# Half A's weights: one clamp of the weight conversion moves from VectorE in PSUM to GpSimd in SBUF

## The chip, the cores and the metric

The kernel runs on one core of a Trainium2 chip. The metric is the device time of one execution in microseconds (us). Such times are given as the median of several runs; a separate execution was profiled, and every row below is from that one.

## The reference

The inputs are q, k, v (batch 4, 8 heads, 576 positions, 64 per head), a threshold tau, and four weight matrices, moe_w_in and moe2_w_in (512 x 2048) and moe_w_out and moe2_w_out (2048 x 512). The matrices arrive as float64, and the kernel reads each number as a pair of 32-bit words. What is computed:

```
scores = (q @ k^T) / sqrt(64);  keep those >= rowmax - tau, set the others to -1e9
attn   = exp(scores - rowmax);  attn /= sum(attn) + 1e-9;  x = (attn @ v) as (2304, 512)
h = x @ w_in;    g = h * clip(h + 3, 0, 6) / 6;   x = g @ w_out
h = x @ w2_in;   g = h - tanh(h);                 out = g @ w2_out
```

## The kernel before

TensorE multiplies each number as a high and a low part, so every product is three passes.

**Stages.** Attention runs over 144 units, each one block of 128 queries (or a left-over block) of one head. For a unit TensorE makes the scores (L678) into one of two PSUM score buffers `s`. VectorE takes the row maximum (L683), ScalarE the exponential into `e` (L685), and VectorE masks it against the threshold (L694), which is the last reader of the score buffer. Two units form a group: ScalarE rounds the group's probabilities to a high half `pp` (L699), GpSimd subtracts to get the low half (L705), SP issues a transposing DMA into `pt` (L708), and TensorE multiplies with v (L731). The first feed-forward layer's hidden units are split into half A (1024 of them) and half B. Half A runs between the attention units (`layer1`, L489 and L850), as batches of queries become complete. Half B and the second feed-forward layer follow after the attention, from about 480 us.

**Half A's weights.** They come as 16 blocks, 8 of `w_in` (tiles `ai`) and 8 of `w_out` (tiles `ao`), each 128 x 512 numbers of 64 bits. `load_w` (L388) converts one block. SP loads the raw words into `st` (3 buffers, L406 and L411). ScalarE writes the magnitude of the upper words, taken as float32 (L414). Four VectorE steps follow: a clamp of the magnitude to the range of float32 (L418), a shift with a mask (L420), sign and exponent from the raw upper word (L423), and the last bits from the lower word, back into `st` (L426). `hi_lo` then splits the float32 number: ScalarE writes the high part (L448), GpSimd the low part (L451). For half A the magnitude and the steps L418 to L423 live in a PSUM buffer `m` (`scratch=R_m`, two buffers, shared with the products of `layer1`). For all other weights they live in `wu` in SBUF (`R_wu`, two buffers), and those blocks come later than 480 us.

**Order of the work.** Every operation is recorded with `add` as a task with an engine, an assumed duration, a key and what it reads and writes. `Plan.issue` then simulates the engines with these durations, lets each free engine take the ready task with the lowest key, and writes the instructions in the order in which they start. Each engine afterwards executes its own list in exactly that order and waits at an instruction whose inputs aren't there. A duration or a dependency that changes can thus move any later instruction of any engine. Half A's blocks have keys that place them among the attention units. The assumed durations that bear on the change are 0.65 us for a VectorE step of half A and `t_pool(512)` = 0.14 + 512 x 0.0021 = 1.215 us for a GpSimd pass over 512 elements.

Of the kernel before, what the change touches and what calls it, by code (L numbers as in the profile page):

```python
# [9 lines left out]
F32 = mybir.dt.float32  # L10
F32R = mybir.dt.float32r
F16 = mybir.dt.float16
I32 = mybir.dt.int32
U32 = mybir.dt.uint32
BF16 = mybir.dt.bfloat16
ACTF = mybir.ActivationFunctionType
ALU = mybir.AluOpType
# [55 lines left out]
class Plan:  # L73
# [13 lines left out]
    def add(self, eng, dur, key, fn, r=(), w=(), after=(), xfer=0.0, hold=False, slack=0.0, port=None):  # L87
        r, w = ([getattr(b, "of", b) for b in x] for x in (r, w))
        deps = dict.fromkeys(after)
        for b in r:  # L90
            deps.update(dict.fromkeys(b.writers))
        t = Task(eng, dur, key, fn, deps, xfer, hold, slack, eng == "pool" if port is None else port)
        t.w = w
        users = dict.fromkeys((*r, *w))
        t.free = [b for b in users if b.ring.free]
        for b in users:
            b.users.append(t)
        for b in w:
            b.writers.append(t)
        self.tasks.append(t)  # L100
        return t
# [86 lines left out]
def t_act(n, sbuf=False, scalars=False):  # L188
    return 0.05 + n / 1200.0 + 0.043 * sbuf + 0.094 * scalars
# [6 lines left out]
def t_pool(n):  # L196
    return 0.14 + n * 0.0021
# [3 lines left out]
def attention_moe_moe_kernel(  # L201
# [29 lines left out]
    nc = tc.nc  # L231
    B, H, S, D = q.shape
    DM = H * D
# [12 lines left out]
    TINY = 2.0 ** -15  # L246
    HUGE = 122879.9921875
# [8 lines left out]
    add = plan.add  # L256
# [122 lines left out]
    R_wu = Ring(2, lambda i: st_p.tile([128, DM], I32, tag=f"wu{i}", name="wu"), free=True)  # L379
# [8 lines left out]
    def load_w(kind, m, src, key, step, to, after=(), slack=0.0, scratch=None, cs=0.0, first=None, low="pool",  # L388
               found=None, put=None):

        wst, wu = R_st.new(), (scratch or R_wu).new()
        f0 = m * 128
        raw = lambda i: wst.t.rearrange("p (n t) -> p n t", t=2)[:, :, i]  # L400
        part = lambda dt: wu.t.bitcast(dt)
        split_, staged = isinstance(to, list), isinstance(to, (Buf, View))

        def load():
            if kind == "i":
                nc.sync.dma_start(  # L406
                    out=wst.t.rearrange("p (k n) -> p k n", k=KD),
                    in_=src[:, 2 * f0:2 * (f0 + 128)].rearrange("(k p) f -> p k f", p=128),
                )
            else:  # L410
                nc.sync.dma_start(out=wst.t, in_=src[f0:f0 + 128, :])  # L411

        add("dma", 0.47, key, load, w=[wst], after=after, xfer=1.75, slack=slack)
        add("act", t_act(DM, sbuf=True), key + 3, lambda: nc.scalar.activation(  # L414
            out=part(F32), in_=raw(1).bitcast(F32), func=ACTF.Abs), r=[wst], w=[wu, to] if staged else [wu],
            slack=cs if first is None else first)
        steps = [
            lambda: nc.vector.tensor_scalar(  # L418
                out=part(F32), in0=part(F32), scalar1=TINY, scalar2=HUGE, op0=ALU.max, op1=ALU.min),
            lambda: nc.vector.tensor_scalar(  # L420
                out=part(I32), in0=part(I32), scalar1=3, scalar2=0x3FFFFFF8,
                op0=ALU.logical_shift_left, op1=ALU.bitwise_and),
            lambda: nc.vector.scalar_tensor_tensor(  # L423
                out=part(I32), in0=raw(1), scalar=-0x40000000, in1=part(I32),
                op0=ALU.bitwise_and, op1=ALU.bitwise_or),
            lambda: nc.vector.scalar_tensor_tensor(  # L426
                out=raw(1).bitcast(U32) if split_ else to.t.bitcast(U32) if staged else part(U32), in0=raw(0).bitcast(U32), scalar=29, in1=part(U32),
                op0=ALU.logical_shift_right, op1=ALU.bitwise_or),
        ]
        for n, f in enumerate(steps):  # L430
            add("dve", 0.65 if n > 1 or scratch else 0.5, key + 3 + n * step, f,
                r=[wu] if n < 2 else [wu, wst], w=[wst] if n == 3 and split_ else [to] if n == 3 and staged else [wu], slack=cs, port=not scratch)
        if staged:
            return wu
        if not split_:
            if found is not None:
                found(wu, key + 3 + 4 * step)
            return add("dma", 0.47, key + 3 + 4 * step, lambda: nc.sync.dma_start(out=to, in_=part(F32)), r=[wu], xfer=0.8)
        n = DM // len(to)
        for h, W in enumerate(to):  # L440
            f32 = lambda h=h: raw(1)[:, h * n:(h + 1) * n].bitcast(F32)
            (hi_lo if put is None else put)(f32, W, [wst], key + 3 + 4 * step, step, n, cs, low)
        return to
# [421 lines left out]
    with tc.manual_schedule():  # L865
# [4 lines left out]
            out=tau_b[:, 2:3], in0=tau_b[:, 0:1], scalar1=0.0, scalar2=scale, op0=ALU.is_ge, op1=ALU.mult,  # L870
# [72 lines left out]
        for u in range(NU + LAG + XL + 4):  # L943
            if u >= LOOK and (u - LOOK) % LOOKS == 0 and wb_parts:
                look(*wb_parts.pop(0), when(u), pend[u - 6].writers[-1:])
            while rounds and rounds[0][0] <= u:
                at_u, r = rounds.pop(0)
                record_round(r, when(at_u))
            if wa_parts:
                kind, m = wa_parts.pop(0)  # L950
                n = 2 * MH - len(wa_parts) - 1
                WA[kind, m] = load_w(
                    kind, m, w1_in if kind == "i" else w1_out, T0 + STEP * (W0 + WS * n + WO * (kind == "o")), 0.8,
                    [R_w[kind, m].new()], slack=ST, scratch=R_m, cs=CS)[0]
            if u < NU:
                pend[u] = softmax(u, when(u))
            if 0 <= u - LAG < NU and sum_group(u - LAG)[-1] == u - LAG:
                weighted(u - LAG, when(u) + PVK, pend[u - LAG])
# [132 lines left out]
        for kind in "io":  # L1091
            mx, k0 = wmax["b" + kind], start - FW - 6.0
            top = add("dve", 0.15, k0, lambda mx=mx: nc.vector.tensor_reduce(
                out=mx[:, 0:1], in_=mx[:, 5:5 + MH], axis=AX.X, op=ALU.max), after=seen[kind])
# [41 lines left out]
        for o, (kind, src) in enumerate((("i", w1_in), ("o", w1_out))):  # L1136
            for m in range(MH):
                W = WB[kind, m] = (R_bw if kind == "i" else R_bo).new()
                load_w(kind, MH + m, src, start - FW + WBO + WBS * (MH * o + m), 0.8, [W], late, cs=CB, first=CB1,
                       put=scaled_pair(wmax["b" + kind][:, 2:3], scaled["b" + kind], kind == "o"))  # L1140
        key = T2
# [7 lines left out]
        for i, ms in work:  # L1149
            c, n = blocks[i]  # L1150
# [21 lines left out]
            if ms[-1] == MH - 1:  # L1172
                y = load_y(i, key - 10.0)
                for h in range(KD // 2):
                    last = add("dve", t_dve(2 * n, scalars=True), key + 2 * PM, lambda h=h, y=y, acc=acc, n=n, i=i: nc.vector.scalar_tensor_tensor(  # L1175
                        out=y.t[:, 2 * h:2 * h + 2, 0:n], in0=acc[h].t[:, 0:2 * n].rearrange("p (d n) -> p d n", d=2),
                        scalar=unscale[:, 1, i:i + 1], in1=y.t[:, 2 * h:2 * h + 2, 0:n], op0=ALU.mult, op1=ALU.add),
                        r=[acc[h], y], w=[y], after=x_ready[i][1])
# [6 lines left out]
                    out=y2[i], in_=y.t[:, :, 0:n]), r=[y], xfer=1.5)  # L1185
# [30 lines left out]
        def to_dram(i, gate, key):  # L1216
            kind, m = wd_parts[i]
            q = quarter(m)
            mx, c = wmax[f"{kind}{q}"], m % (2 * MQ)

            def found(wu, k):
                f32 = lambda: wu.t.bitcast(F32)
                junk = View(R_t2.new(), lambda t: t.bitcast(BF16)[:, 0:DM])
                x = row_sums(f32, mx[:, 5 + c:6 + c], lambda: junk.t, [wu], [junk], k, DM, CL)
                w_found.setdefault((kind, q), []).append(x)

            wd_stores[kind, m] = load_w(
                kind, m, w2_in if kind == "i" else w2_out, key, 0.8, wd[kind, m], [gate], slack=0.2, cs=CL, first=CF,
                found=found)
# [237 lines left out]
        for idx, st in enumerate(order2):  # L1467
# [7 lines left out]
            n = NB  # L1475
# [121 lines left out]
```

## Time and profile before

| | |
|---|---|
| three timed runs | 1088.57, 1094.69, 1092.71 us; median 1092.71 |
| the profiled execution | 1088.51 us; its span from first to last instruction 1086.7 us |
| TensorE matmul busy | 1015.0 us (93%) |
| VectorE busy | 847.6 us (78%) |
| ScalarE busy | 718.6 us (66%) |
| GpSimd busy | 339.0 us (31%) |
| mean granted TensorE clock | 0.964 |

PE is TensorE's matmul, PEld its weight load, DVE VectorE, ACT ScalarE, POOL GpSimd, SP the engine that issues most DMAs. Busy shares are averages over stages with different limits. The page cuts the span into 40 equal slices of 27.2 us and gives each engine's busy share in tenths, and the granted TensorE clock in tenths of full speed:

```profile
PE   5668799999999899988999999999999999999998
DVE  5889977687869788758797778889976796784564
ACT  6867979687967786645675566756755675574332
POOL 2656757666855675623000000000001111121000
PEclk8668899999999989998999999999999999999999
```

### The profile page before, as it was taken

To read this page: it belongs to the slowest core of one execution; us is meant where nothing else is said; L and a number is where in the kernel's file an instruction comes from. 1 tells how busy PE (TensorE), PEld (TensorE's weight loads), DVE (VectorE), ACT (ScalarE), POOL (GpSimd) and SP (SyncE) were. 2 spreads that over 40 slices of the span, in tenths; PEclk is the share of its full clock that TensorE was granted. 3 is DMA by queue.
4 is the path that set the end of the run, shared out by engine and by line. 5 is a ranking of instruction groups with operands and counts; after the bars stand their busy time and mean duration, and the time that the engine had idled before them with its cause. 6 is when DMAs were issued, how large, how long until landed. Compare 5 with 4: busy or idle time off the path is not lost.

```text
span 1086.7 us, 23294 instructions
## 1 busy us (share of the span) xinstructions
PE 1015.0 (93%) x8984; PEld 838.6 (77%) x8984; DVE 847.6 (78%) x1630; ACT 718.6 (66%) x1312; POOL 339.0 (31%) x353
## 2 busy tenths in 40 slices
PE   5668799999999899988999999999999999999998
PEld 4557788998999799978988888876676666666664
DVE  5889977687869788758797778889976796784564
ACT  6867979687967786645675566756755675574332
POOL 2656757666855675623000000000001111121000
PEclk8668899999999989998999999999999999999999
DMA  7899688967899989978657755432333866573335
GB/s 184 165 222 213 132 159 182 196 132 158 187 181 192 205 175 216 219 159 261 201 173 257 253 199 185 165 108 97 107 117 118 208 131 117 126 127 51 87 92 142
DMA packets 285007, 179.27 MB, mean 165 GB/s; under 512 B 202976, under 2 KB 257760, under 8 KB 284896
## 3 DMA queue, kind: packets, MB, share of 16 engines
q1 hardware_dynamic: 279088, 168.07, 61.0%
q0 software_dynamic: 5184, 9.44, 6.5%
q8 instruction: 71, 1.16, 0.5%
q14 instruction: 40, 0.33, 0.1%
q10 hardware_dynamic: 624, 0.26, 0.1%
HBM read 89.13 MB, written 46.14 MB: 124 GB/s over the span
## 4 chain that ended last, share of the span: by engine, by line
PE 58%; DVE 4%; ACT 1%; DMA 1%; issue 0%; SPq 0%; ACTq 0%; DVEq 0%
PE ya L489 24%; PE m L489 16%; PE h L489 10%; PE m L850 3%; PE s L678 2%; PE tp L731 1%; DMA y<-y 1%; PE h L850 1%; PE m L476 0%; DVE x L1276 0%; DMA st<-in_moe_w_in_dram 0%; DVE xh L1048 0%; DVE t L803 0%; PE tp L561 0%; DVE y L1175 0%
## 5 line engine op out<-in xcount | busy, mean ns | idle before, releaser
L705 POOL TENSOR_TENSOR pp<-e,pp 128x128 f16<-128x128 f32 (+3 forms) x156 | 181.1, 1182 | 120.3 <-issue 54.1
L489 PE MATMUL ya<-wo,g 128*128 128x512 f16 x864 | 205.4, 379 | 1.0 <-DVE g L813 0.6
L489 PEld LDWEIGHTS <-wi 128*128 128x128 f16 x1536 | 150.0, 98 | 40.4
L1416 POOL DMA_DIRECT2D po<-o x36 | 31.2, 876 | 459.7 <-ACT o L1410 459.7
L489 PEld LDWEIGHTS <-g 128*128 128x128 f16 x864 | 84.1, 98 | 79.3 <-DVE g L813 1.1
L683 DVE TENSOR_REDUCE z<-s 128x1 f32<-128x576 f32 x144 | 107.9, 753 | 45.4 <-PE s L678 44.7
L694 DVE SCALAR_TENSOR_TENSOR e<-s,z,e 128x576 f32<-128x576 f32 x144 | 115.8, 811 | 22.1 <-ACT e L685 17.1
L678 PE MATMUL s<-ks,q 128*128 128x288 f32 x512 | 105.9, 337 | 20.9 <-DVE e L694 20.1
L685 ACT ACTIVATE e<-s,z 128x576 f32<-128x576 f32 x144 | 105.0, 739 | 26.6 <-DVE z L683 20.3
L489 PE MATMUL m<-xT,ai 128*128 128x256 f32 (+1 forms) x720 | 112.8, 301 | 1.8 <-DVE st L426 0.6
L678 PEld LDWEIGHTS s<-ks,q 128*128 128x128 f32 x512 | 82.4, 212 | 29.4 <-DVE e L694 13.4
L489 PEld LDWEIGHTS m<-xT,ai 128*128 128x128 f32 x720 | 99.3, 190 | 3.7 <-DVE st L426 1.1
L489 PE MATMUL ya<-g,bo 128*128 128x256 f16 x864 | 101.1, 273 | 0.5 <-DVE g L813 0.5
L731 PE MATMUL tp<-vt,pt 128*128 128x65 f16 (+1 forms) x2240 | 88.4, 199 | 8.5 <-ACT q L591 2.4
L489 PE MATMUL m<-x,wi 128*128 128x256 f16 x768 | 95.2, 273 | 0.0
L731 PEld LDWEIGHTS <-pt 128*128 128x128 f16 (+1 forms) x2240 | 79.8, 104 | 16.7 <-DMA pt<-pp 6.0
L1381 ACT ACTIVATE t<-t,hid_s 128x512 f32<-128x512 f32 x72 | 51.6, 718 | 62.0 <-DVE t L1372 61.4
L489 PEld LDWEIGHTS <-bo 128*128 128x128 f16 x864 | 84.1, 98 | 10.6 <-issue 0.9
L489 PEld LDWEIGHTS <-bw 128*128 128x128 f16 x864 | 84.1, 98 | 10.4 <-issue 0.4
L813 DVE SCALAR_TENSOR_TENSOR g<-g,t 128x512 f16<-128x512 f16 x108 | 73.8, 686 | 20.7 <-ACT g L809 20.2
L809 ACT ACTIVATE g<-t 128x512 f16<-128x512 f32 x108 | 67.0, 624 | 33.7 <-DVE t L1383 26.0
L699 ACT ACTIVATE pp<-e 128x1152 f16<-128x1152 f32 (+1 forms) x80 | 85.1, 1064 | 5.0 <-DVE e L694 4.7
(177 smaller groups left out, 1878.0 us busy)
## 6 DMA issues: line engine op xcount, KB each, us to landing
st<-in_moe_w_in_dram SPq DMA_DIRECT2D x40, 512.0 KB, 5.0
st<-in_moe_w_out_dram SPq DMA_DIRECT2D x40, 512.0 KB, 4.4
xf<-xs SPq DMA_DIRECT2D x18, 512.0 KB, 5.2
y<-y SPq DMA_DIRECT2D x18, 512.0 KB, 3.8
po<-o POOLq DMA_DIRECT2D x36, 256.0 KB, 4.2
xs<-xT SPq DMA_DIRECT2D x8, 640.0 KB, 4.9
y<-ys SPq DMA_DIRECT2D x9, 512.0 KB, 5.9
po<-o SPq DMA_DIRECT2D x18, 256.0 KB, 2.0
```

The lines of the kernel that those rows point to most:

```text
L489: nc.tensor.matmul(ps, l[a], r[b], start=first and t == 0 and i == 0, stop=last and t == 2 and i == n - 1,)
L678: nc.tensor.matmul(ps.t[:, half, 0:SH], l, ks[:, half * SH:(half + 1) * SH], start=i == 0, stop=i == len(ops) - 1,)
L683: add("dve", 0.69, key, lambda: nc.vector.tensor_reduce(out=z.t[:, 0:1], in_=s(), axis=AX.XY, op=ALU.max, negate=True), r=[ps], w=[z])
L685: exp = add("act", 0.66, key, lambda: nc.scalar.activation(out=ex(), in_=s(), func=ACTF.Exp, bias=z.t[:, 0:1]), r=[ps, z], w=[e])
L694: add("dve", 0.74, key, lambda: nc.vector.scalar_tensor_tensor(out=ex(), in0=s(), scalar=z.t[:, 1:2], in1=ex(), op0=ALU.is_ge, op1=ALU.mul ...
L699: high = add("act", t_act(w * S, sbuf=True), key, lambda: nc.scalar.activation(out=pp.t[:, 0:w, 0:S], in_=e.t[:, 0:w, :], func=ACTF.Copy), ...
L705: add(eng, dur, key, lambda src=src, dst=dst, queue=queue: queue.tensor_tensor(out=pp.t[:, 0:w, dst], in0=e.t[:, 0:w, src], in1=pp.t[:, 0: ...
L731: nc.tensor.matmul(pv.t[0:m, w_ * (D + 1):(w_ + 1) * (D + 1)], pt.t[:, n, blk, rows], vv, start=o == 0, stop=o == len(ops) - 1)
L809: hi = add("act", t_act(n, sbuf=True), key, lambda: nc.scalar.activation(out=gh(), in_=t(), func=ACTF.Copy, scale=GS2 if far else 1.0), r= ...
L813: go = lambda: nc.vector.scalar_tensor_tensor(out=gl(), in0=gh(), scalar=1.0 / GS2, in1=t(), op0=ALU.mult, op1=ALU.subtract)
L850: prev = [add("pe", t_mm(n, 1), kd, lambda p=p, l=l, r=r, m=m, s=s, ps=ps: nc.tensor.matmul(ps.t[:, 0:n], W["o", m].t[:, l, s], r[m].t[:, ...
L1381: add("act", t_act(2 * NB, sbuf=True, scalars=True), key, lambda: nc.scalar.activation(out=s_(), in_=h.t, func=ACTF.Tanh, scale=c), r=[h], ...
```

## The change

For half A alone (`scratch` given) the magnitude gets a tile of its own, `mag`, from the SBUF ring `R_wu`. ScalarE writes it there. The clamp is one GpSimd instruction in place in that tile, its minimum first and its maximum second. The VectorE clamp L418 is left out for half A, and the shift reads `mag` and writes the PSUM buffer, which half A takes from that step on. For all other weights `mag` is `wu`, and nothing differs.

```diff
         wst, wu = R_st.new(), (scratch or R_wu).new()
+        mag = R_wu.new() if scratch else wu
...
+        size = lambda dt: mag.t.bitcast(dt)
         add("act", t_act(DM, sbuf=True), key + 3, lambda: nc.scalar.activation(
-            out=part(F32), in_=raw(1).bitcast(F32), func=ACTF.Abs), r=[wst], w=[wu, to] if staged else [wu],
+            out=size(F32), in_=raw(1).bitcast(F32), func=ACTF.Abs), r=[wst], w=[mag, to] if staged else [mag],
             slack=cs if first is None else first)
+        if scratch:
+            add("pool", t_pool(DM), key + 3, lambda: nc.gpsimd.tensor_scalar(
+                out=size(F32), in0=size(F32), scalar1=HUGE, scalar2=TINY, op0=ALU.min, op1=ALU.max), r=[mag], w=[mag])
         steps = [
-            lambda: nc.vector.tensor_scalar(
+            None if scratch else lambda: nc.vector.tensor_scalar(
                 out=part(F32), in0=part(F32), scalar1=TINY, scalar2=HUGE, op0=ALU.max, op1=ALU.min),
             lambda: nc.vector.tensor_scalar(
-                out=part(I32), in0=part(I32), scalar1=3, scalar2=0x3FFFFFF8,
+                out=part(I32), in0=size(I32), scalar1=3, scalar2=0x3FFFFFF8,
                 op0=ALU.logical_shift_left, op1=ALU.bitwise_and),
...
         for n, f in enumerate(steps):
+            if f is None:
+                continue
             add("dve", 0.65 if n > 1 or scratch else 0.5, key + 3 + n * step, f,
-                r=[wu] if n < 2 else [wu, wst], w=[wst] if n == 3 and split_ else [to] if n == 3 and staged else [wu], slack=cs, port=not scratch)
+                r=[mag] if n < 2 else [wu, wst], w=[wst] if n == 3 and split_ else [to] if n == 3 and staged else [wu], slack=cs, port=not scratch)
```

## Rows read from the trace of the kernel before

**Rows 1.** Stretches: length, busy us of each engine (instructions), clock, DMA share, GB/s.
```profile
20.00:140.00 120.00, 88.50 (x825) 77.19 (x826) 107.86 (x181) 96.03 (x194) 80.84 (x76) 0.74 0.83 175
140.00:480.00 340.00, 325.46 (x3665) 309.02 (x3663) 261.81 (x511) 257.16 (x492) 210.65 (x213) 0.99 0.87 181
480.00:1086.70 606.70, 591.53 (x4458) 444.96 (x4458) 468.51 (x916) 353.69 (x607) 43.91 (x46) 0.99 0.54 152
```

**Rows 2.** The same view in slices of 20 us: PE, PEld, DVE, ACT, POOL.
```profile
40.00:60.00 20.00, 13.60 (x118) 11.94 (x118) 16.80 (x29) 16.01 (x32) 15.20 (x13) 0.66 0.99 198
60.00:80.00 20.00, 12.46 (x90) 10.58 (x90) 17.75 (x28) 13.01 (x26) 10.81 (x10) 0.57 0.96 214
80.00:100.00 20.00, 15.09 (x158) 13.05 (x159) 18.27 (x30) 14.69 (x29) 13.94 (x14) 0.74 0.86 200
100.00:120.00 20.00, 17.69 (x192) 15.85 (x192) 19.63 (x34) 17.96 (x43) 14.78 (x15) 1.00 0.93 191
120.00:140.00 20.00, 14.64 (x165) 13.87 (x164) 16.59 (x29) 16.14 (x34) 14.79 (x15) 0.83 0.62 113
```

**Rows 3.** Waits of PE and DVE, 20 to 140: us in total, times, longest.
```profile
PE s L678 <- DVE e L694: 18.9, 13, 4.9
...
DVE z L683 <- PE s L678: 3.2, 10, 0.8
DVE m L418 <- ACT m L414: 2.8, 3, 1.6
```

**Rows 4.** Lines L418, L426: ns min/median/max, first and last start, form.
```profile
L418 DVE TENSOR_SCALAR wu<-wu x48: 404/419/524, 487.5 to 923.5; 128x512 f32<-128x512 f32 x48
L418 DVE TENSOR_SCALAR m<-m x16: 680/690/700, 23.3 to 127.8; 128x512 f32<-128x512 f32 x16
...
L426 DVE SCALAR_TENSOR_TENSOR st<-st,m x16: 629/677/680, 34.4 to 132.0; 128x512 uint32<-128x512 uint32 x16
```

**Rows 5.** VectorE in order of time: start us, us, instruction.
```profile
76.20 0.69 DVE L418 TENSOR_SCALAR m<-m 128x512 f32<-128x512 f32 x1
76.80 0.81 DVE L694 SCALAR_TENSOR_TENSOR e<-s,z,e 128x576 f32<-128x576 f32 x1
```

**Rows 6.** GpSimd's groups, 20 to 140: busy us, mean ns | idle before.
```profile
L705 POOL TENSOR_TENSOR pp<-e,pp 128x1024 f16<-128x1024 f32 x16 | 34.2, 2138 | 0.0
L451 POOL TENSOR_TENSOR ao<-st,ao 128x512 fp32r<-128x512 f32 x8 | 10.5, 1308 | 5.3 <-ACT ao L448 5.3
...
L705 POOL TENSOR_TENSOR pp<-e,pp 128x512 f16<-128x512 f32 x3 | 3.5, 1163 | 0.0
L554 POOL COPY qr<-qr 128x256 f32<-128x256 f32 x8 | 3.2, 404 | 0.0
```

**Rows 7.** Waits of SP's queue, 20 to 140.
```profile
SPq L708 <- POOL pp L705: 3.9, 4, 1.6
```

**Rows 8.** ScalarE: the two forms of L414, and a wait, 20 to 140.
```profile
L414 ACT ACTIVATE wu<-st x48: 648/666/704, 486.8 to 922.4; 128x512 f32<-128x512 f32 x48
L414 ACT ACTIVATE m<-st x16: 608/624/647, 19.9 to 127.0; 128x512 f32<-128x512 f32 x16
...
ACT e L685 <- POOL pp L705: 2.0, 2, 1.3
```

**Rows 9.** Waits of GpSimd for ScalarE and VectorE, 20 to 140.
```profile
POOL pp L705 <- ACT pp L699: 10.0, 4, 5.2
POOL gl L816 <- ACT gh L809: 5.5, 5, 2.2
POOL ao L451 <- ACT ao L448: 5.3, 4, 2.5
POOL ai L451 <- ACT ai L448: 4.6, 4, 2.1
...
POOL vt L644 <- ACT vt L642: 0.7, 1, 0.7
POOL x L778 <- DVE rx L766: 0.5, 1, 0.5
```

## The prediction

> **What bounds the kernel now.** I read three views in turn: busy time by stretch, then the waits inside the stretch that the change touches, then the order of instructions on single engines.
>
> Busy time first [rows 1]. From 140 us on, TensorE is the bound: 325.46 of 340 us busy until 480, and 591.53 of the 606.7 us after it, both at a granted clock of 0.99. Nothing of half A's weight work lies there, so the change can alter that part only by letting it begin sooner or later. The stretch from 20 to 140 us is another kernel: TensorE 88.50 of 120 us, VectorE 107.86, ScalarE 96.03, GpSimd 80.84. The reader is to see that VectorE is the fullest engine, and, slice by slice, that it leads in each of the five slices from 40 us on, with 16.59 to 19.63 us of 20 [rows 2]. TensorE's granted clock is 0.57 to 0.74 in the first three of them, a mean between its levels of 1.2 and 2.4 GHz.
>
> The waits say the same. In this stretch TensorE's scores wait 18.9 us for VectorE's masking step L694, 13 times, because that step gives the score buffers back; VectorE's own longest waits are 3.2 and 2.8 us in sum [rows 3]. So VectorE sets the pace of the attention units up to 140 us, TensorE sets it afterwards, and the 16 weight blocks of half A lie wholly inside the first part: L418 runs from 23.3 to 127.8 us [rows 4].
>
> **The change, part by part.**
>
> *Removed.* 16 VectorE clamps in PSUM, of 690 ns median [rows 4]. An instruction on this engine begins before the records let its predecessor end: the clamp at 76.20 is followed by the next instruction at 76.80 [rows 5], so one clamp takes 0.60 us of the queue. 16 x 0.60 = 9.6 us. VectorE was busy for 107.86 of 120 us, 90%; I count 90% of this as path, 8.6 us.
>
> *Added on GpSimd.* 16 one-input passes of 128x512 float32 in SBUF. No row shows this operation. The nearest is the copy L554, 128x256 float32 in 404 ns: also one input, one output, half the size. Doubled it gives 0.81 us. With a fixed part taken off it is less: the two sizes of L705, 1163 ns for 512 and 2138 ns for 1024 elements, differ by 1.90 ns per element and leave 0.19 us fixed, so the copy costs 0.84 ns per element and 512 of them 0.62 us. The upper bound is the two-input subtraction of the same shape, L451 with 1308 ns [rows 6]. A second arithmetic step rides in the same pass; I take 0.75 us, near the copy, and keep 0.62 to 1.31. 16 x 0.75 = 12.0 us on an engine that is idle for 39.2 of the 120 us. Below nothing it can't be: the engine gains work and loses none.
>
> The Trainium skill's "GPSIMD Engine Reference", section "Engine selection", speaks against such a move: elementwise work belongs on VectorE, GpSimd being about twice as slow with two inputs, though near line rate with one. Its section "Elementwise — side-by-side cycle accounting" gives 769 ns for 512 elements in its best loop, by which the 16 would be 12.3 us, an estimate from that page; no run here shows it.
>
> *The wait that moves.* VectorE waited 2.8 us, three times, for the magnitudes [rows 3]. That wait now falls on GpSimd, which takes its work in a written order: behind a clamp that waits for L414 stand the low halves of the probabilities (L705), the low halves of the weights (L451) and the query copies (L554). For L705 wait the transposing DMAs of SP, which wait 3.9 us on it now [rows 7], and behind those the next loads of SP, q, k and the raw weights among them; ScalarE's exponentials L685 wait for L705 to give back its e buffer, 2.0 us in two waits [rows 8]. I expect this last wait to double, and charge 2.0 us. VectorE's shift L420 gets a wait for GpSimd instead of ScalarE. Behind it on VectorE stand the softmax steps L683 and L694, so a late clamp stalls them; the written order puts the shift where a clamp of 1.2 us is done, more than I assume, and I charge nothing. If that cover fails, each late clamp costs up to its own 0.75 us.
>
> *Rerouted operands.* The magnitudes go to SBUF instead of PSUM: 666 against 624 ns [rows 8], 16 x 0.042 = 0.7 us on ScalarE, which is 80% busy and hides it. The shift L420 now reads SBUF and writes PSUM. With both ends in PSUM such a step takes 690 ns, with both in SBUF 419 [rows 4]; the mixed case is not shown. I take the first, no change; the second would give 16 x 0.27 = 4.3 us more. Half A's PSUM buffer is held from the shift instead of from the magnitudes, which can only free it earlier for layer 1, whose products share the two buffers; I count nothing for it. The two SBUF buffers of the magnitudes are otherwise used from 486.8 us on [rows 8], so no one else waits for them.
>
> The Trainium skill's "VectorE: DVE Perf Modes", section "Why PSUM operands drop a tier", holds that any PSUM operand keeps float32 at the single rate. The two forms of L418 agree with it at their ends, 419 and 690 ns; by it the mixed shift stays at the slow price and the extra 4.3 us don't come.
>
> *Sum.* 8.6 - 2.0 = 6.6 us earlier at 140 us. After that TensorE is 96% and 98% busy [rows 1] on work that stays the same, so I let the gain pass to the end whole. The profiled execution took 1088.51 us (its span of 1086.7 and 1.8 around it): 1081.9. The median of the three timed runs is 1092.71, 4.2 above the profiled one; I forecast against the median: 1086.1, as 1086.
>
> **The rivals.**
>
> *GpSimd ties VectorE, nothing moves.* GpSimd's idle 39.2 us are not all free. 26.6 of them are waits for ScalarE and VectorE in six lines, 10.0 + 5.5 + 5.3 + 4.6 + 0.7 + 0.5 [rows 9]. If those waits stay as long, 12.6 us are free, and 16 clamps at 0.79 us fill them: the stretch keeps its 120 us although VectorE got lighter. 1092.7. For it speaks how close 0.79 lies to 0.75; against it that most of these waits are for producers that VectorE itself holds up, and so should shrink.
>
> *GpSimd becomes the bound: slower.* The same queue, with the clamp at the price of L451. 16 x 1.31 = 20.9 us against 12.6 free: the stretch grows by 8.3 us, to 1101.0. The place is L705 behind the clamps, seen as waits of L685 and of the transposes. It decides from 0.79 us per clamp upward if the waits stay. For it: in the slice from 40 to 60 us GpSimd is at 15.20 of 20 and gets three clamps, 3.9 us at that price, so 19.1; from 100 to 120, 14.78 and 3.9 [rows 2]. Against it: one input instead of two.
>
> *The shift gets cheap too.* Should L420 run at its SBUF price, 4.3 us come on top: 1081.8. Nothing shows VectorE at that rate with one end in PSUM.
>
> *The change does less than it says.* All later instructions are placed anew by the planner from its own prices, so layer 1's products may fall otherwise among the units. TensorE idles for 31.5 us between 20 and 140 and for 14.5 until 480 [rows 1]; an order that is worse by a few waits of 1 to 2 us blurs every case. I hold that in the widths, not as a case.
>
> **How the numbers follow.** The forecast has 0.46, its own range 1080 to 1091; the tie 0.29; the slower case 0.19; the cheap shift 0.06. About 0.5%, 5.5 us, is what a measurement of this kernel can tell from no change: faster than 1087.2 are the cheap shift and 0.40 of the forecast, 0.46; within it the tie and 0.06 of the forecast, 0.35; slower than 1098.2 the last case, 0.19. The range 1077 to 1100 leaves out about half of the slower case and a little below the cheap shift.
>
> **What would show it right or wrong.** Right: VectorE's busy time from 20 us to the last ao block falls by some 11 us, that last block is done about 6 us sooner than now (its L426 begins at 132.0 us, [rows 4]), and the stretch behind it has the same length. The clamp's mean shows which case holds: under 0.79 us the first two, above it the slower. Wrong in its main step if VectorE's busy share in this stretch drops well below 90% with no gain in time, its idle time ended by GpSimd or by TensorE's scores; wrong in its second if the stretch gets shorter and the part after 140 us gives it back. It fails outright if L685 or the transposes wait more than 8 us for L705.

## The result and the profile after

The changed kernel took 1105.91 us (median of 4 runs, 1103.27 to 1107.32) against 1091.55 us of the kernel before on the same chip (4 runs): a ratio of 1.0139, 95% interval 1.0110 to 1.0169. It is slower by 1.4%. The forecast was 1086 us with a range of 1077 to 1100. The profiled execution took 1103.27 us, with a span of 1101.5 (before 1086.7).

In the changed kernel's line numbers the magnitude is L416, the clamp L420, the shift L425 and the last bits L431; scores, row maximum, exponential and mask are L685, L690, L692 and L701; layer 1's first products (x with `ai`) are L496, its second ones (the gated result with `ao`) L857. The four weight lines first, from the view of one line: instruction and count, ns min/median/max, first and last start.

```profile
L416 ACT ACTIVATE wu<-st x16: 652/661/682, 20.2 to 135.2; 128x512 f32<-128x512 f32 x16
...
L420 POOL TENSOR_SCALAR wu<-wu x16: 610/613/619, 20.9 to 136.6; 128x512 f32<-128x512 f32 x16
...
L425 DVE TENSOR_SCALAR m<-wu x16: 676/684/695, 23.6 to 138.5; 128x512 int32<-128x512 int32 x16
...
L431 DVE SCALAR_TENSOR_TENSOR st<-st,m x16: 678/679/690, 31.1 to 140.6; 128x512 uint32<-128x512 uint32 x16
```

The moved clamp is cheap and the shift costs what it did. But L431 begins for the last time at 140.6 us, where [rows 4] had 132.0. Busy time by stretch, the rows that answer to [rows 1], and one part of them:

```profile
20.00:140.00 120.00, 88.45 (x784) 78.43 (x784) 101.24 (x170) 98.30 (x197) 87.18 (x91) 0.74 0.82 181
140.00:480.00 340.00, 319.63 (x3540) 303.65 (x3541) 254.93 (x493) 249.33 (x478) 211.04 (x213) 0.97 0.83 174
480.00:1101.50 621.50, 604.80 (x4622) 457.97 (x4620) 477.40 (x930) 359.05 (x618) 44.72 (x48) 0.99 0.54 151
...
140.00:180.00 40.00, 35.43 (x363) 34.08 (x364) 21.86 (x40) 24.95 (x53) 19.93 (x19) 0.87 0.65 142
```

The last row has this counterpart in the kernel before:

```profile
140.00:180.00 40.00, 38.30 (x432) 35.90 (x430) 30.55 (x55) 34.54 (x74) 24.70 (x24) 1.00 0.82 179
```

VectorE lost 6.6 us of work up to 140 us, and TensorE is exactly as busy there as before, 88.45 against 88.50 at 0.74. Most of the loss is right behind: from 140 to 180 us TensorE is busy for 35.43 instead of 38.30 us, at a granted clock of 0.87 instead of 1.00. Busy time times clock is 30.8 against 38.3 us, so 7.5 us of full-speed work are missing. From 180 to 480 us TensorE is busy for another 3 us less, 284.20 against 287.16 us, at the same clock of 0.99. The units say the same. Counted by the starts of the row maximum, with the first unit as number 0, unit 28 is 2.5 us ahead of the kernel before, unit 36 is 2.6 us behind, unit 44 is 10.0 behind, the last one 11.9 and the end 14.8. The waits from 20 to 140 us, for [rows 3]:

```profile
DVE z L690 <- PE s L685: 9.8, 13, 1.9
...
PE s L685 <- DVE e L701: 15.8, 18, 2.6
```

VectorE now waits 9.8 us for scores, not 3.2. What happens at 140 us is seen in the order of time, TensorE first (start, us, instruction; in brackets the idle time before it and what ended it):

```profile
140.73 0.80 PE L685 MATMUL s<-ks,q 128*128 128x288 f32 x4 [2.23 <-DVE e L701]
143.65 3.38 PE L738 MATMUL tp<-vt,pt 128*64 128x65 f16 x56 [2.12 <-DVE ks L593]
146.84 3.25 PE L857 MATMUL m<-gh,ao 128*128 128x256 f32 x16
149.93 1.12 PE L857 MATMUL m<-gl,ao 128*128 128x256 f32 x8
150.89 2.08 PE L857 MATMUL m<-gh,ao 128*128 128x256 f32 x16
...
154.71 0.69 PE L685 MATMUL s<-ks,q 128*128 128x288 f32 x4
```

```profile
142.02 0.76 DVE L690 TENSOR_REDUCE z<-s 128x1 f32<-128x576 f32 x1
...
154.55 0.68 DVE L770 SCALAR_TENSOR_TENSOR rx<-x,sv 128x16 f32<-128x16 f32 x1 [7.82 <-ACT x L745]
...
155.43 0.76 DVE L690 TENSOR_REDUCE z<-s 128x1 f32<-128x576 f32 x1
```

And TensorE in the kernel before, at its first second products:

```profile
136.69 2.15 PE L850 MATMUL m<-gh,ao 128*128 128x256 f32 x16
138.68 1.12 PE L850 MATMUL m<-gl,ao 128*128 128x256 f32 x8
139.63 0.69 PE L678 MATMUL s<-ks,q 128*128 128x288 f32 x4
140.16 1.35 PE L850 MATMUL m<-gh,ao 128*128 128x256 f32 x10
```

Before, scores stand between the second products. After, the second products begin 10 us later, the first 16 of them take 3.25 instead of 2.15 us, and no scores come from 140.73 to 154.71: a hole of 13.4 us between the maxima of two units, 142.02 to 155.43. The longest hole of the kernel before among units 30 to 48 is 7.6 us. This hole is a sight, not yet a cause; s1 below tests it.

### The profile page after: what moved, and what is told of

It reads as the page before. It is cut to its first block, busy times and chain, and to the rows that moved or that the text cites. A ratio compares the mean times of both kernels' runs of the same rounds, so it can differ in the third digit from the quotient of the medians.

```text
span 1101.5 us, 23287 instructions
## 1 busy us (share of the span) xinstructions
PE 1022.7 (93%) x8984; PEld 847.8 (77%) x8984; DVE 842.7 (77%) x1614; ACT 718.2 (65%) x1312; POOL 346.5 (31%) x369
## 4 chain that ended last, share of the span: by engine, by line
PE 75%; DVE 5%; ACT 4%; DMA 1%; issue 1%; POOL 1%; SPq 0%; ACTq 0%; POOLq 0%; DVEq 0%
PE ya L496 24%; PE m L496 19%; PE h L496 10%; PE m L857 8%; PE s L685 5%; PE tp L738 4%; PE tp L568 1%; DVE z L690 1%; PE h L857 1%; DVE e L701 1%; ACT e L692 1%; PE m L483 1%; DMA pt<-pp 1%; DMA f<-wdi 1%; ACT pp L706 0%
## 5 line engine op out<-in xcount | busy, mean ns | idle before, releaser
L712 POOL TENSOR_TENSOR pp<-e,pp 128x128 f16<-128x128 f32 (+3 forms) x156 | 180.9, 1180 | 120.1 <-ACT pp L706 57.9
L496 PE MATMUL ya<-wo,g 128*128 128x512 f16 x864 | 205.4, 379 | 1.4 <-ACT g L816 0.8
L496 PEld LDWEIGHTS <-wi 128*128 128x128 f16 x1536 | 150.0, 98 | 40.4
L690 DVE TENSOR_REDUCE z<-s 128x1 f32<-128x576 f32 x144 | 108.1, 754 | 53.7 <-PE s L685 52.3
L496 PEld LDWEIGHTS <-g 128*128 128x128 f16 x864 | 84.1, 98 | 79.6 <-ACT g L816 1.2
L701 DVE SCALAR_TENSOR_TENSOR e<-s,z,e 128x576 f32<-128x576 f32 x144 | 116.3, 812 | 22.8 <-ACT e L692 10.7
L685 PE MATMUL s<-ks,q 128*128 128x288 f32 x512 | 107.8, 339 | 25.7 <-DVE e L701 25.3
L692 ACT ACTIVATE e<-s,z 128x576 f32<-128x576 f32 x144 | 105.2, 738 | 24.8 <-DVE z L690 20.2
L496 PE MATMUL m<-xT,ai 128*128 128x256 f32 (+1 forms) x720 | 114.3, 304 | 2.5 <-DVE t L810 1.1
L685 PEld LDWEIGHTS s<-ks,q 128*128 128x128 f32 x512 | 84.2, 215 | 33.8 <-DVE e L701 17.6
L496 PEld LDWEIGHTS m<-xT,ai 128*128 128x128 f32 x720 | 101.0, 193 | 4.2 <-DVE t L810 2.0
L738 PE MATMUL tp<-vt,pt 128*128 128x65 f16 (+1 forms) x2240 | 91.5, 202 | 12.9 <-DVE q L600 2.9
L496 PE MATMUL ya<-g,bo 128*128 128x256 f16 x864 | 101.6, 273 | 0.7 <-DVE g L820 0.7
L738 PEld LDWEIGHTS <-pt 128*128 128x128 f16 (+1 forms) x2240 | 82.7, 106 | 21.5 <-issue 10.6
L496 PE MATMUL m<-x,wi 128*128 128x256 f16 x768 | 95.2, 273 | 0.0
L496 PEld LDWEIGHTS <-bo 128*128 128x128 f16 x864 | 83.8, 98 | 10.8 <-issue 1.1
L496 PEld LDWEIGHTS <-bw 128*128 128x128 f16 x864 | 84.4, 98 | 10.0
L816 ACT ACTIVATE g<-t 128x512 f16<-128x512 f32 x108 | 66.9, 624 | 30.8 <-DVE t L1390 26.1
```

The source lines that it names most:

```text
L496: nc.tensor.matmul(ps, l[a], r[b], start=first and t == 0 and i == 0, stop=last and t == 2 and i == n - 1,)
L685: nc.tensor.matmul(ps.t[:, half, 0:SH], l, ks[:, half * SH:(half + 1) * SH], start=i == 0, stop=i == len(ops) - 1,)
L690: add("dve", 0.69, key, lambda: nc.vector.tensor_reduce(out=z.t[:, 0:1], in_=s(), axis=AX.XY, op=ALU.max, negate=True), r=[ps], w=[z])
L692: exp = add("act", 0.66, key, lambda: nc.scalar.activation(out=ex(), in_=s(), func=ACTF.Exp, bias=z.t[:, 0:1]), r=[ps, z], w=[e])
L701: add("dve", 0.74, key, lambda: nc.vector.scalar_tensor_tensor(out=ex(), in0=s(), scalar=z.t[:, 1:2], in1=ex(), op0=ALU.is_ge, op1=ALU.mul ...
L712: add(eng, dur, key, lambda src=src, dst=dst, queue=queue: queue.tensor_tensor(out=pp.t[:, 0:w, dst], in0=e.t[:, 0:w, src], in1=pp.t[:, 0: ...
```

## The experiments

All ran against the kernel before on their own chip. The ratio is the recorded one with its 95% interval; it is not the quotient of the medians that the paragraphs give (for l2 that quotient is 1.0109). The other columns are read from the one profiled execution of each kernel, and executions of one kernel scatter by several us: the 23 of the kernel before beside e4 lie between 1087.94 and 1095.53 us. "Last block" is the end of the 16th low half of half A's weights, "second" the start of the second products, "hole" the longest time between two maxima from unit 30 to 48, "TensorE" its busy time times granted clock from 140 to 180 us.

| kernel | ratio, 95% interval | last block | second | hole | unit 44 | TensorE |
|---|---|---|---|---|---|---|
| before | 1 | 136.4 | 136.7 | 7.6 | 164.6 | 38.3 |
| after | 1.0139 (1.0110 to 1.0169) | 143.3 | 146.8 | 13.4 | 174.6 | 30.8 |
| e1, order of before, clamp on GpSimd | 0.9984 (0.9969 to 1.0000) | 135.7 | 136.1 | 7.1 | 164.0 | 38.3 |
| e2, order of after, clamp on VectorE | 1.0163 (1.0133 to 1.0193) | 146.3 | 149.8 | 12.8 | 178.4 | 28.0 |
| e3, order of before, GpSimd clamp early | 1.0020 (1.0003 to 1.0038) | 136.5 | 138.4 | 7.9 | 166.3 | 38.3 |
| e4, order of before, no clamp | 1.0008 (0.9991 to 1.0024) | 134.1 | 135.8 | 8.2 | 163.7 | 38.3 |
| l1, before priced 0.60 | 1.0078 (1.0049 to 1.0106) | 141.9 | 143.3 | 8.8 | 173.0 | 36.5 |
| l2, after priced 0.61 | 1.0084 (1.0055 to 1.0113) | 149.7 | 152.0 | 18.6 | 173.4 | 31.8 |
| l3, before priced 0.70 | 1.0155 (1.0113 to 1.0196) | 144.6 | 145.5 | 7.2 | 172.7 | 32.8 |
| s1, after, scores moved into the hole | 1.0121 (1.0091 to 1.0151) | 141.6 | 146.2 | 8.4 | 172.9 | 31.5 |
| m1, after, half A in SBUF | 1.0182 (1.0161 to 1.0203) | 155.8 | 156.4 | 9.9 | 182.7 | 27.9 |
| m1b, before, half A in SBUF | 1.0219 (1.0195 to 1.0243) | 151.3 | 153.5 | 10.2 | 184.0 | 30.2 |
| m3, after, PSUM taken early | 1.0109 (1.0081 to 1.0137) | 154.5 | 152.8 | 13.1 | 175.2 | 31.4 |
| t1, after, keys 7.5 | 1.0049 (1.0026 to 1.0072) | 141.2 | 144.3 | 12.0 | 166.1 | 35.6 |
| t2, after, keys 10.5 | 1.0098 (1.0078 to 1.0118) | 147.9 | 148.3 | 13.2 | 177.9 | 29.1 |
| t3, after, keys 11 | 1.0082 (1.0054 to 1.0110) | 144.4 | 145.3 | 12.8 | 167.0 | 37.2 |
| t4, before, keys 7 | 1.0052 (1.0033 to 1.0072) | 135.9 | 136.2 | 7.1 | 168.9 | 37.8 |
| h1, after, first products held | 1.0069 (1.0044 to 1.0094) | 146.8 | 147.3 | 12.5 | 169.7 | 34.7 |
| h2, t1, first products held | 1.0050 (1.0029 to 1.0070) | 140.3 | 142.2 | 13.1 | 169.1 | 34.9 |
| h3, t1, last two held | 1.0045 (1.0026 to 1.0063) | 143.0 | 145.5 | 11.3 | 169.0 | 35.9 |

**e1 and e2: the hop, or the order?** In e1 the planner sees the tasks of the kernel before, and so writes its order; only the instruction at the place of VectorE's clamp goes to GpSimd, and the magnitude lies in SBUF as in the changed kernel. In e2 it sees those of the changed kernel, and the clamp's place in that order is filled by VectorE. In the traces the instructions of VectorE, ScalarE and GpSimd, clamps aside, stand in e1 exactly as in the kernel before, and in e2 exactly as in the changed kernel.

```diff
 e1 (against after):
...
-        if scratch:
-            add("pool", t_pool(DM), key + 3, lambda: nc.gpsimd.tensor_scalar(
...
-            None if scratch else lambda: nc.vector.tensor_scalar(
+            lambda: (nc.gpsimd if scratch else nc.vector).tensor_scalar(
...
 e2 (against after):
-            add("pool", t_pool(DM), key + 3, lambda: nc.gpsimd.tensor_scalar(
+            add("pool", t_pool(DM), key + 3, lambda: nc.vector.tensor_scalar(
```

> The written order of all engines is that of the kernel before; only the 16 clamps leave VectorE's list and stand in GpSimd's, at the point where VectorE had them. Theory 'order' (the loss comes from the new order that the planner wrote, not from the clamp on GpSimd): VectorE's 9.6 us are relieved and nothing else moves, so 1083 to 1091 us. Theory 'hop' (the loss comes from the clamp standing in GpSimd's queue between ScalarE and VectorE at run time): 1100 us or more, as with the change.

> The written order is that of the changed kernel; only the clamp goes back to VectorE, in SBUF, at the point where GpSimd had it. Theory 'order': the time stays near the changed kernel's, 1100 to 1108 us. Theory 'hop': without the clamp on GpSimd it returns to that of before, 1088 to 1094 us, less up to 4 us because the SBUF clamp takes 419 instead of 690 ns.

1089.32 us for e1, 1109.23 for e2. The order alone makes the change slow: with it the kernel is slow without GpSimd's clamp, and without it GpSimd's clamp costs nothing. It brings next to nothing either. The rows of e1 from 20 to 140 us, by stretch, by waits and by GpSimd's groups:

```profile
20.00:140.00 120.00, 87.13 (x830) 76.43 (x831) 99.33 (x166) 96.63 (x194) 90.01 (x92) 0.75 0.85 176
```

```profile
DVE m L422 <- POOL wu L420: 8.6, 8, 2.2
DVE z L685 <- PE s L680: 6.7, 12, 1.9
```

```profile
L420 POOL TENSOR_SCALAR wu<-wu 128x512 f32<-128x512 f32 x16 | 9.8, 615 | 2.2 <-ACT wu L416 2.2
```

VectorE has 8.5 us less to do than in [rows 1] and waits 8.6 us for the clamps, where it waited 2.8 us for the magnitudes in [rows 3], and 6.7 instead of 3.2 us for scores.

**e3 and e4: is VectorE's relief worth anything?** e3 keeps the order of before and puts the GpSimd clamp right behind the magnitude, so that VectorE needn't wait so long for it. e4 leaves half A's clamps out altogether; its magnitudes aren't limited.

```diff
 e4 (against before):
-            lambda: nc.vector.tensor_scalar(
+            lambda: None if scratch else nc.vector.tensor_scalar(
```

> As e1_old_order, but each GpSimd clamp stands right behind its magnitude in the written order instead of where VectorE had the clamp. In e1 VectorE's shift waited 8.6 us in 8 waits for the clamp, nearly the 9.6 us that were taken off it. Theory 'the hop ate the relief': those waits fall under 3 us and the time goes to 1081 to 1086 us. Theory 'VectorE's time was not the path' (a unit's pace is set by the written order and the handoffs, so a lighter VectorE only idles): 1087 to 1091 us, as e1.

> The kernel before without half A's 16 clamps at all (the magnitudes are not limited to the range; all else and the written order are as before). It prices the relief by itself. If VectorE's 9.6 us are path, 1081 to 1085 us; if VectorE only idles instead, 1087 to 1091 us.

1093.52 and 1090.96 us: no gain, even with the clamps gone. In e3 VectorE still waited 5.2 us for the clamps, where under 3 was expected, and the time is 0.2% up, above both ranges; e4 is the clean test, and it lies in the range for a VectorE that only idles. e4 from 20 to 140 us:

```profile
20.00:140.00 120.00, 88.14 (x833) 77.28 (x834) 100.16 (x167) 96.62 (x197) 80.80 (x76) 0.77 0.84 180
```

```profile
DVE z L683 <- PE s L678: 8.5, 16, 1.9
DVE e L694 <- ACT z L688: 6.4, 12, 1.4
...
PE s L678 <- DVE e L694: 19.4, 13, 3.8
```

The second line was this in the kernel before:

```profile
DVE e L694 <- ACT z L688: 2.2, 5, 0.8
```

VectorE's work falls by 7.7 us and its waits in these two lines rise by 9.5 (from 3.2 and 2.2), while its wait of 2.8 us for the magnitudes is gone. TensorE's wait for the mask stays at 19.4 (18.9 in [rows 3]). The two engines and ScalarE pass a unit round a ring of score buffers; here, taking work from one of them lengthens its own waits and hardly shortens the round. In the profiled execution of e4 units are 2.3 us ahead at number 36, 0.9 at 44, and the last one is 2.3 us behind.

**l1, l2, l3: does any other order cost as much?** These change only the planner's assumed price of one step, so the instructions are the same and the order isn't.

```diff
 l1, l3 (against before; 0.70 in l3):
-            add("dve", 0.65 if n > 1 or scratch else 0.5, key + 3 + n * step, f,
+            add("dve", 0.60 if scratch else 0.65 if n > 1 else 0.5, key + 3 + n * step, f,
 l2 (against after):
-            add("pool", t_pool(DM), key + 3, lambda: nc.gpsimd.tensor_scalar(
+            add("pool", 0.61, key + 3, lambda: nc.gpsimd.tensor_scalar(
```

> The kernel before, with one number of the planner changed: a VectorE step of half A is assumed at 0.60 us (its measured pitch) instead of 0.65. No instruction is added, removed or moved to another engine; only the written order differs. Theory 'order': such a re-ordering alone can move the time by more than 5 us either way, to 1080 to 1086 or 1097 to 1106. Theory 'hop': order hardly matters, 1088 to 1095 us.

> The changed kernel, with the planner's price of the GpSimd clamp at its measured 0.61 us instead of 1.215. The same instructions on the same engines in another written order. Theory 'order': the time leaves 1105.9 by more than 5 us. Theory 'hop': the clamp still stands in GpSimd's queue, 1102 to 1109 us.

> The kernel before with half A's VectorE steps assumed at 0.70 us by the planner, all instructions the same in another written order. Theory 'order': the order of before is one of many, most of them slower; another draw gives 1096 to 1106 us. Rival (order matters only through half A's lateness): with half A assumed slower the attention is planned further ahead, 1090 to 1096 us.

1099.73, 1103.23 and 1108.09 us. A price that is 0.05 us off costs the kernel before 0.8 or 1.6% with no work changed, and the true price of the clamp doesn't repair the changed kernel. l1 lies in the range of its theory 'order', l3 2 us above its own. l2 alone decides nothing: its seven times scatter from 1096.28 to 1104.58 us, and their median lies in the range of theory 'hop'.

**s1: is the hole the cause?** After's order, with the softmax steps of units 38 and 39 written ahead of the run of second products.

```diff
 s1 (against after):
...
+        ahead([("scores", 38)], first)
+        ahead([("max", 38), ("exp", 38), ("z", 38), ("mask", 38)], third)
+        ahead([("scores", 39)], third)
+        ahead([("max", 39), ("exp", 39), ("z", 39), ("mask", 39)], stop)
...
```

> The changed kernel in its written order, with one edit: scores, maximum, exponential and mask of units 38 and 39 are written ahead of the uninterrupted run of layer 1's second products behind which they stood. Theory 'lump' (the new order puts layer 1's overdue products ahead of the scores, so VectorE had nothing for 7.8 us at 146 us): that wait falls under 4 us, unit 40 begins 4 to 6 us sooner, 1099 to 1103 us. Rival (the loss is spread over many small waits and the clock): no gain, 1104 to 1108 us.

1104.43 us. The hole shrank from 13.4 to 8.4 us, yet units 36 to 44 still took 36.7 us, as in the changed kernel (29.3 before). Undoing the hole alone brings next to nothing, as the rival had it. Nor does a loss need a long hole: l3 is 1.55% slower with one of 7.2 us, shorter than that of the kernel before.

**m1, m1b, m3: is half A held up for a PSUM buffer?** Half A takes its buffer `m` later now, when layer 1's products may hold both. m1 and m1b keep half A out of PSUM; m3 takes the buffer as early as before.

```diff
 m1 (against after):
-        wst, wu = R_st.new(), (scratch or R_wu).new()
-        mag = R_wu.new() if scratch else wu
+        wst, wu = R_st.new(), R_wu.new()
+        mag = wu
 m1b (against before):
-        wst, wu = R_st.new(), (scratch or R_wu).new()
+        wst, wu = R_st.new(), R_wu.new()
 m3 (against after):
-            ... r=[wst], w=[mag, to] if staged else [mag],
+            ... r=[wst], w=[mag, to] if staged else [mag, wu] if scratch else [mag],
```

> The changed kernel with half A's magnitudes, clamps and shifts wholly in SBUF: the shift writes over the magnitude instead of into a PSUM buffer m, so half A's blocks no longer share m with layer 1's products. Theory (half A's last block comes late because its shift must find a free m; TensorE then runs out of products before 140 us): the last L431 instruction ends by 137 us (after 140.6, before 132.0 by the same reading), layer 1's second products start by 139 us (after 146.8), and the time is within 0.5% of the kernel before, 1086 to 1096 us. Rival (any written order other than the one of the kernel before is slower, wherever the last block lies): 1099 to 1108 us.

> The kernel before with half A wholly in SBUF: the clamp stays on VectorE, but works on the magnitude's own SBUF tile, and the shift too, so no PSUM buffer m is taken by half A. Theory (m is what holds half A back): the last L429 instruction ends at or before 132 us, and the time is 1082 to 1092 us. Rival (any other written order is slower): 1099 to 1108 us.

> The changed kernel, with the PSUM buffer m of a block of half A already taken when ScalarE writes the magnitude (as the kernel before takes it), though only the shift writes into it. By the plan that this makes, half A's last block comes no earlier than in the changed kernel. Theory (the time follows the last block): last block done at 145 us or later and 1103 to 1112 us. Rival (the later taking of m is the loss by itself): 1088 to 1096 us.

1110.50, 1114.98 and 1101.59 us. Out of PSUM the last block comes later, not earlier (155.8 and 151.3 us), so the expectation that freeing the buffer brings it forward failed. But each of the three is a new order as well, so the buffer's own part isn't separated from the order's. m3 also weakens the theory that the time follows the last block: it comes 11 us later than in the changed kernel, and the time is no longer (1.0109 against 1.0139); it lies outside both ranges of m3.

**t1 to t4: the change, or one order?** Three other orders of the changed kernel and one of the kernel before, through the keys of half A's blocks.

```diff
 t1 (against after); t2: 10.5, 0.8, -2.0; t3: 11.0, 1.0, -2.0; t4 (against before): 7.0, 0.8, -2.0
-    W0, WS, WO = 8.0, 0.8, -2.0
+    W0, WS, WO = 7.5, 0.6, -1.0
```

> The changed kernel with other keys for half A's blocks (W0, WS, WO 7.5, 0.6, -1 for 8, 0.8, -2), so that the planner writes another order with the same work. Theory (the change itself costs nothing; the kernel before merely has an order that few other keys reach): orders scatter, this one lies anywhere from 1088 to 1110 us, and among the three re-keyed changed kernels at least one comes within 0.5% of the kernel before. Rival (half A with a clamp on GpSimd in between keeps its raw buffers longer in every order, so the last block is late and the time at least 1% up): 1101 us or more in all three, last block done at 141 us or later.

> The changed kernel with keys 10.5, 0.8, -2. By its plan the second products start earliest of the changed kernels' orders (3.3 us before the changed kernel's). Late-block theory: last block done 3 us before that of the changed kernel (143.3) and the time some 5 us below it, near 1100 us; theory of scatter: anywhere from 1088 to 1110 us.

> The changed kernel with keys 11, 1.0, -2, a third order. Scatter: 1088 to 1110 us, whatever its last block; rival: 1101 us or more with the last block at 141 us or later.

> The kernel before (clamp on VectorE in PSUM) with keys 7.0, 0.8, -2: by its plan the second products start 3.7 us earlier than in the kernel before. Late-block theory: last block done by 133 us (136.4 before) and the time at or below that of the kernel before, 1083 to 1092 us. Scatter: slower than before by 0.5 to 2%, 1097 to 1112 us, in spite of an earlier last block.

1096.36, 1100.41, 1099.62 and 1095.35 us. A better order takes back two thirds of the loss; none of the three is level with the kernel before. The rival of t1, 1101 us or more in all three, failed; t1, at 1.0049, is just within the 0.5% that its theory asked for. The planner's times don't come true on the chip: t2's second products, planned 3.3 us earlier than in the changed kernel, came 1.5 us later, and its last block 4.6 us later, so t2 doesn't test the late block. t4, the old work in a new order, is 0.5% slower although its last block and its second products come no later; it lies between both of its ranges. The late block isn't needed for a loss. t1's early units do show VectorE's relief, 5.2 us ahead at unit 16 and 4.4 at unit 36, and lose it to 1.6 behind at unit 44, with a hole of 12.0 us.

**h1 to h3: TensorE without products.** In the changed orders layer 1's first products end 23 to 35 us before the second ones begin (31.5 in the changed kernel, 13.9 before). These runs hold the later of the eight first products back until a block of half A's output weights is written.

```diff
 h1 (against after); h2 (against t1): W["o", 4]; h3 (against t1): W["o", 3] and m == 6
-            prev = turn[-1:]
+            prev = turn[-1:] + (W["o", 2].writers if (b, g) == (0, 0) and m == 4 else [])
```

> The changed kernel, with the fifth of layer 1's eight first products (0,0) held until half A's output block 2 is written, so that the last four fall into the time in which TensorE had none. Theory (the changed orders finish the first products long before half A's last block, and TensorE's time in between is unused): the gap between the end of the first products and the start of the second ones falls from 31.5 us to 20 us or less, units 36 to 44 take 33 us or less (36.7 in the changed kernel, 29.3 before), and the time falls to 1093 to 1100 us. Rival (an order's time is scatter, not set by this gap): units 36 to 44 stay at 35 us or more, or the time stays at 1101 to 1110 us with a shorter gap.

> The re-keyed changed kernel t1 (1096.4 us), with its fifth first product held until half A's output block 4. Theory: gap from 31.3 us to 20 us or less, units 36 to 44 from 35.2 us to 32 us or less, time 1087 to 1094 us, which would be level with the kernel before. Rival: no faster than t1, 1095 to 1106 us.

> The re-keyed changed kernel t1, with only the last two first products held, until half A's output block 3. Theory: half of what h2 brings, gap 20 to 26 us, 1089 to 1096 us. Rival: 1095 to 1106 us.

1098.57, 1096.62 and 1095.61 us. h1 gained 0.7% against the changed kernel, but its gap stayed at 30.4 us, so not by way of the gap. In h2 the gap halved to 15.0 us, near that of the kernel before, and the time is no better than t1's. h3, with a gap of 24.6 us, lies in both of its ranges. And l1, l3, m1b and t4 are slow with gaps of 3.6, 11.6 and 11.1 us and, in t4, none. So the gap isn't what an order's time follows. TensorE in h2:

```profile
124.91 2.28 PE L496 MATMUL m<-xT,ai 128*128 128x256 f32 x12
...
142.21 3.76 PE L857 MATMUL m<-gh,ao 128*128 128x256 f32 x16
...
147.16 2.08 PE L857 MATMUL m<-gh,ao 128*128 128x256 f32 x16
...
150.97 0.69 PE L685 MATMUL s<-ks,q 128*128 128x288 f32 x4
```

The run of second products ahead of the next scores is still there, and its first 16 products still take long, 3.76 us.

**What all 20 kernels say together.** Much of the difference between kernels is there by unit 44: across them, its start correlates with the median time at 0.91. With the start of the second products it is 0.83, with the last block 0.77, with the gap of h1 to h3 0.26. These numbers say where a loss is seen, not what causes it. No version beats both kernels; e1 is level with the kernel before.

## Why the prediction was wrong

**"Removed": 90% of VectorE's 9.6 us counted as path, 8.6 us.** This step failed. With the order held still, taking the clamps away is worth nothing (e4: 1.0008, 0.9991 to 1.0024), and moving them to GpSimd is worth 0.16%, 1.7 us, with an interval that reaches to nothing (e1: 0.9984, 0.9969 to 1.0000). The interval of e4 leaves at most 0.09%, 1.0 us, of the 8.6. A share of 90% busy was read as 90% on the path. The waits of [rows 3] were read from one side only: TensorE waiting for the mask step showed that VectorE is a link of the ring, not that it is the only one. The prediction's own sign came true: VectorE's busy time dropped without a gain, and its idle time was ended by TensorE's scores, 9.8 us.

**"The wait that moves", 2.0 us.** This charge didn't come as stated: ScalarE's wait for the low halves (L712), which was to double, is gone from its waits of the stretch. What moved is GpSimd's wait for the magnitudes. In the changed kernel it is longer than the 2.8 us that VectorE waited; in e1 it is 2.2 us.

```profile
POOL wu L420 <- ACT wu L416: 8.9, 3, 4.7
```

**"The change does less than it says", held in the widths and not as a case.** This is where the sign was lost. The prediction said that the planner would place all later instructions anew and priced that at "a few waits of 1 to 2 us". The order cost 1.6% with the clamp on VectorE (e2), and 0.8 and 1.6% when only a price moved by 0.05 us (l1, l3). It should have been a case of its own on the slower side: fifteen orders other than that of the kernel before were run, eleven of them with the clamp on GpSimd, and all fifteen are slower, by 0.45 to 2.2%. The kernel before has an order that is better than its neighbours.

**"I let the gain pass to the end whole."** Wrong as well. In the changed kernel the units were ahead up to number 28 and behind from 32 on, at the change from VectorE's stretch to TensorE's. In e4, with the order held, the 2.3 us of unit 36 were gone at the last unit.

**The slower rival, "GpSimd becomes the bound"**, gave 1101.0, near the result, by a mechanism that the runs don't bear out. One clamp took 0.614 us, under its point of decision (0.79) and even a little under the lower bound of 0.62. Neither of its marks shows: ScalarE's wait for L712 is gone, and SP's transposes wait 2.0 us for those low halves, less than the 3.9 of [rows 7]. One part of it is there under other names: behind all of GpSimd's operations together the transposes wait 41.7 us, 30.9 in the kernel before, and some of that is behind the clamp itself.

```profile
SPq L715 <- POOL wu L420: 4.5, 2, 3.1
```

This isn't the cause either: e1 carries the same GpSimd work, its transposes wait 37.7 us, 8.7 of them behind the clamp, and it loses nothing.

**What held.** The clamp's price was 0.75 in the sum and 0.614 in the trace. The magnitude took 661 ns, where 666 was taken. The shift with its input in SBUF and its output in PSUM took 684 ns; "no change" was right. The Trainium skill's "VectorE: DVE Perf Modes", section "Why PSUM operands drop a tier", holds that any PSUM operand keeps float32 at the single rate; the trace agrees for this 32-bit integer step, 684 ns. The Trainium skill's "GPSIMD Engine Reference", section "Elementwise — side-by-side cycle accounting", gives 769 ns for 512 elements in its best loop; the trace has 614, and the measurement decides.

**What stays open.** Why one order is worth 1% more than another isn't settled. Shown is the place: units 28 to 44, around the start of the second products, where TensorE of the changed kernel does 7.5 us less full-speed work. Three single features were tested by taking them away, the PSUM buffer, the hole and the gap, and none brought the time back; for the buffer and the gap the order changed too. The delay of the last block can be read from the loads: a raw buffer `st` is held for 20.9 us from the issue of its load to the low half (19.6 before), and 16 blocks through 3 buffers make 1.27 x 16 / 3 = 6.8 of the 6.9 us. That is worked out, not shown by a run; and e1, with the same hop, holds its buffers for 19.6 us, so the hop alone doesn't lengthen it.

## What to carry to other kernels

An engine that is 90% busy in a ring of three engines need not be the path: before pricing a relief, ask who waits for it and what it will wait for next, and try it with the work left out and the order held still. Where a planner or a scheduler writes the order, an edit is two changes, the work and a new order; separate them by emitting the new instruction in the old order, and be ready for a new order of a tuned kernel to be worse: here all fifteen were, by 0.45 to 2.2%.

## What the hardware showed beyond expectation

A one-input pass of GpSimd with two arithmetic steps over 128x512 float32 took 610 to 619 ns in SBUF, less than VectorE's 690 ns for the same step in PSUM, though more than its 419 with both ends in SBUF [rows 4].

And a stretch with idle TensorE was followed by slow products. From 120 to 140 us of the changed kernel TensorE was busy for 13.16 of 20 us, at a granted clock of 0.69. From 142.5 to 149.3 us the clock was 0.50, and the first 16 second products, begun at 146.84, took 3.25 us. In the kernel before TensorE was busy for 14.64 us from 120 to 140 us, at 0.83 [rows 2]; its clock was 1.00 from 134.3 us on, and the first 16 second products, begun at 136.69, took 2.15 us. That the idle time brought the low clock is read from the order of events; no run varied it alone. Rows of the changed kernel, with the clock in the third column from the end (1.00 is 2.4 GHz, 0.50 is 1.2), then one of the kernel before:

```profile
120.00:140.00 20.00, 13.16 (x121) 11.50 (x118) 15.91 (x27) 16.03 (x32) 14.68 (x17) 0.69 0.82 170
...
142.50:149.30 6.80, 5.65 (x67) 5.61 (x68) 2.89 (x5) 2.94 (x9) 3.88 (x5) 0.50 0.48 94
```

```profile
134.30:144.00 9.70, 9.63 (x141) 9.53 (x140) 5.54 (x8) 5.09 (x12) 6.36 (x7) 1.00 0.86 141
```
